# A zero-tile warm-up of TensorE from the first microsecond, and token tile 2's transposes moved behind the first slot

## The chip, the cores and the metric

The kernel runs on 1 core of a Trainium2 chip. The metric is the device time of one execution in microseconds (us), so less is better. Executions of one kernel differ by 1 to 3.5 us within a group of runs (2.1 us over 45 runs of the kernel before on one chip, 3.5 us over 62 on another), which is more than the change moves, so distributions are compared as well as medians.

## The reference, cut to what matters

A linear attention with cosine weights feeds a two-layer MLP with a squared ReLU.

```python
q_p = concat(relu(q) * cos_w, relu(q) * sin_w)      # 8 batches, 8 heads, 576 tokens, 64 -> 128 features
k_p = concat(relu(k) * cos_w, relu(k) * sin_w)
kv  = einsum('bhsf,bhsd->bhfd', k_p, v);  z = k_p.sum(axis=2)
x   = (q_p @ kv) / (q_p @ z + 1e-6)                 # -> 4608 tokens x 512
h   = x @ w_in                                      # 512 -> 2048
out = (relu(h) ** 2) @ w_out                        # 2048 -> 512
```

## The kernel before

All the work of TensorE is one stream of "slots". A batch has a first matmul stage (`gemm1`, against `w1sb`) and a second (`gemm2`, against `w2sb`). The attention of later batches is hung behind slots. Batch 0 has nothing in front of it to hide behind; its attention is the front that the change is about: k and v give `kz`, q is transposed (`tq`), multiplied (`num`), divided, transposed again (`tx`), and then slot 0 begins. `w1sb` and `w2sb` are the two weight matrices on the chip; each is loaded in four quarters through GpSimd's DMA queue. PSUM is the memory that the matmuls write their sums into; the tags `hps`, `yps` and `pa` in the code name groups of PSUM buffers, and in this kernel a buffer is used again only when VectorE or ScalarE has copied it out (in the first profile the fourth matmul of the second stage starts at 38.78 us, behind VectorE's copies, which take 0.77 us from 37.97).

```python
def warm(j):                                  # matmuls without use, to keep TensorE busy
    wm = ps_h.tile([P, 2, FP], F32, name="wm", tag="hps", bufs=2)
    for i in range(2):
        nc.tensor.matmul(out=wm[:, i, :], lhsT=ident[:, :],
                         rhs=kp_of(0, j)[:, i * HH : (i + 1) * HH, :], ...)

def gemm2(b, s):
    if b == 0:
        if s == 0:                            # four accumulators: two on the hps tag, two on yps
            yh = ps_h.tile([P, 2, DM], F32, name="yh", tag="hps", bufs=2)
            ...
            yps = ps_y.tile([P, DM], F32, name="yps", tag="yps", bufs=2)
        for hb in range(s * HB // 8, (s + 1) * HB // 8):
            for tt in range(J):
                gemm2_mm(b, tt, hb, ypss[b][tt])
        ...

load_batch(0, nc.sync, "kvq")
constants()
for j in range(NS):
    att_k(0, j)
    if j < J:
        warm(j)                               # 8 matmuls on the features of k
att_v(0, J - 1, nc.gpsimd, H - 1, H)          # GpSimd's first copy: it waits for v
...
for i in range(4):
    load_w1(i, 4)                             # GpSimd's queue, in this order
load_batch(1, nc.gpsimd, "qkv")
for i in range(4):
    load_w2(i, 4)
load_batch(2, nc.gpsimd, "qkv")
att_kv(0, 0); att_kv(0, 1)                    # kz
for j in range(J):
    warm(j)                                   # 8 more
...
att_qT_pe(0, 2)                               # transposes of token tile 2, in front of slot 0
att_qT_copy(0, 2, True)
for s in range(len(slots)):
    run(s)
```

Of the kernel before, what the change touches and what calls it, by code (L numbers as in the profile page):

```python
# [12 lines left out]
BF16 = mybir.dt.bfloat16  # L13

EPS = 1e-06
FP = 512
# [3 lines left out]
def kernel(  # L20
# [9 lines left out]
    nc = tc.nc  # L30
    P = nc.NUM_PARTITIONS
# [7 lines left out]
    J = S // P  # L39
    MAIN = J * P  # L40
    TAIL = S - MAIN
    HH = H // 2
# [3 lines left out]
    const = ctx.enter_context(tc.tile_pool(name="const", bufs=1))  # L46
# [35 lines left out]


    ident = const.tile([P, P], BF16, name="ident")
    cos_col = const.tile([P, J + 1], F32, name="cos_col")
    sin_col = const.tile([P, J + 1], F32, name="sin_col")

    def constants():
        sidx = const.tile([P, J + 1], F32, name="sidx")
        for p0, p1, c, n, base, mult in [  # L90
            (0, P, 0, J, 0, J),
            (0, TAIL, J, 1, MAIN, 1),
            (TAIL, P, J, 1, MAIN, 1),
        ]:
            nc.gpsimd.iota(
                sidx[p0:p1, c : c + n],
                pattern=[[1, n]],
                base=base,
                channel_multiplier=mult,
                allow_small_or_imprecise_dtypes=True,  # L100
            )
        bias_pi2 = const.tile([P, 1], F32, name="bias_pi2")
        nc.vector.memset(bias_pi2, math.pi / 2.0)
        theta_scale = (math.pi / 2.0) / S
        nc.scalar.activation(cos_col, sidx, ACTF.Sin, bias=bias_pi2[:], scale=-theta_scale)
        nc.scalar.activation(sin_col, sidx, ACTF.Sin, bias=0.0, scale=theta_scale)
        make_identity(nc, ident)
# [31 lines left out]
    def cached(tiles, key, shape, tag, bufs):  # L139
        if key not in tiles:  # L140
            tiles[key] = att.tile(shape, BF16, name=tag, tag=tag, bufs=bufs)
        return tiles[key]


    def kp_of(b, j):
        if j == J:
            return cached(kps, (b, 1), [P, HH, F], "kpt", 1)
        return cached(kps, (b, 0), [P, J, H, F], "kp", 1)[:, j]
# [12 lines left out]
    def xT_of(b, i):  # L161
        return cached(xts, (b, i), [P, KB, 2 * P], "xT", 4)
# [29 lines left out]
        else:  # L192
            copy(out=vx[:, j, h0:h1, 0:D], in_=piece("v", b, j)[:, h0:h1, :])  # L193

    def warm(j):

        wm = ps_h.tile([P, 2, FP], F32, name="wm", tag="hps", bufs=2)
        for i in range(2):
            nc.tensor.matmul(  # L199
                out=wm[:, i, :],  # L200
                lhsT=ident[:, :],
                rhs=kp_of(0, j)[:, i * HH : (i + 1) * HH, :],
                start=True,
                stop=True,
            )

    def fill(n):

        wm = ps_a.tile([P, 2, FP], F32, name="wm", tag="pa", bufs=1)
        for i in range(n):  # L210
            nc.tensor.matmul(  # L211
                out=wm[:, i % 2, :],
                lhsT=ident[:, :],
                rhs=kp_of(0, 0)[:, 0:HH, :],
                start=True,
                stop=True,
            )
# [52 lines left out]
    def att_qT_pe(b, j, apart=False):  # L270

        nh = H if j < J else HH
        tq = ps_y.tile([P, H, P], BF16, name="tq", tag="yps", bufs=2)
        tqs[b, j] = [tq[:, 0:HH, :]]
        if apart:
            hi = ps_h.tile([P, HH, P], BF16, name="tqh", tag="hps", bufs=2)
            tqs[b, j].append(hi)
        elif nh == H:
            tqs[b, j].append(tq[:, HH:H, :])
        for h in range(nh):  # L280
            nc.tensor.transpose(  # L281
                tqs[b, j][h // HH][:, h % HH, :], qp_of(b, j)[:, h, :], ident[:, :]
            )

    def att_qT_copy(b, j, both=False):
        qpTs[b, j] = []
        for i, tq in enumerate(tqs[b, j]):
            t = att.tile([P, HH, P], BF16, name=f"qpTp{i}", tag=f"qpTp{i}", bufs=5)
            copy = nc.scalar.copy if both and i else nc.vector.tensor_copy
            copy(out=t[:, :, :], in_=tq[:, :, :])  # L290
            qpTs[b, j].append(t)
# [46 lines left out]
            src = xs[b, i].rearrange("p k c -> p (k c)")  # L338
        nc.sync.dma_start_transpose(out=dst, in_=src)

    def att_x_pe(b, j, in_y=False):
        nk = KB if j < J else 2
        if in_y:
            tx = ps_y.tile([P, KB, P], BF16, name="tx", tag="yps", bufs=2)
        else:
            tx = ps_a.tile([P, KB, P], BF16, name="tx", tag="pa", bufs=1)
        for kb in range(nk):
            nc.tensor.transpose(tx[:, kb, :], x_of(b, j)[:, kb, :], ident[:, :])  # L348
        if j < J:
            dst = xT_of(b, j // 2)[:, :, j % 2 * P : (j % 2 + 1) * P]  # L350
        else:
            dst = xT_tails(b // 2)[:, b % 2].rearrange("p k g c -> p k (g c)")
        nc.scalar.copy(out=dst, in_=tx[:, 0:nk, :])



# [2 lines left out]
    def gemm1(b, s):  # L359
        if s == 0:  # L360
            gTs[b] = mlp.tile([P, HB, MAIN], BF16, name="gT", tag="gT", bufs=1)
        if s == 8:
            gTts[b // 2] = mlp.tile([P, HB, 2 * TAIL], BF16, name="gTt", tag="gTt", bufs=1)
        half = s // 4
        w, nh = (2 * P, 4) if half < 2 else (P, 8)
        h0 = s % 4 * nh
        hps = ps_h.tile([P, nh, w], F32, name="hps", tag="hps", bufs=2)

        step = P if (b, s) == (0, 0) else w
        for c in range(0, w, step):  # L370
            for i in range(nh):
                hb = h0 + i
                for kb in range(KB):
                    out = hps[:, i, c : c + step]
                    if half < 2:
                        rhs = xT_of(b, half)[:, kb, c : c + step]
                    else:
                        rhs = xT_tails(b // 2)[:, :, kb % 2, kb // 2, :]
                        out = out.rearrange("p (m c) -> p m c", m=2)
                    nc.tensor.matmul(  # L380
                        out=out,
                        lhsT=w1sb[:, kb, hb * P : (hb + 1) * P],
                        rhs=rhs,
                        start=(kb == 0),
                        stop=(kb == KB - 1),
                    )
        rt = mlp.tile([P, nh, w], BF16, name="rt", tag="rt", bufs=2)
        nc.scalar.activation(out=rt[:, :, :], in_=hps[:, :, :], func=ACTF.Relu)  # L388
        if half < 2:
            dst = gTs[b][:, h0 : h0 + nh, half * w : (half + 1) * w]  # L390
        else:
            dst = gTts[b // 2][:, h0 : h0 + nh, :]

        def square():
            nc.vector.tensor_tensor(out=dst, in0=rt[:, :, :], in1=rt[:, :, :], op=ALU.mult)  # L395

        return square
# [58 lines left out]
    for b in range(B):  # L456
        n = 8 + 2 * (b % 2)
# [4 lines left out]
    def at(s, fn, *args):  # L462
        after.setdefault(s, []).append((fn, args))
# [30 lines left out]
            at(kv[i], att_kv, b, i)  # L494


    at(0, att_qT_pe, 0, 3)
    at(0, att_num, 0, 2)
    at(0, att_qT_copy, 0, 3, True)
    at(0, att_div, 0, 2)  # L500
    at(1, att_x_pe, 0, 2, True)
    at(1, att_d, 0, 3)
    at(2, att_x_pe, 0, 3, True)
    at(12, att_feat, 0, J)
    at(17, att_t, 0, J)
    at(19, att_d, 0, J)
# [45 lines left out]
    with tc.manual_schedule():  # L552
        load_batch(0, nc.sync, "kvq")
        constants()
        for j in range(NS):
            att_k(0, j)
            if j < J:
                warm(j)
        att_v(0, J - 1, nc.gpsimd, H - 1, H)
        att_v(0, 0, nc.vector)  # L560
        att_v(0, 1, nc.scalar)
        att_v(0, 2, nc.vector)
        att_v(0, 3, nc.vector, 0, H - 1)
        att_v(0, J, nc.vector)
        for i in range(4):
            load_w1(i, 4)
# [3 lines that stand above are left out]
        load_batch(2, nc.gpsimd, "qkv")  # L570
        att_kv(0, 0)
        att_kv(0, 1)
        for j in range(J):
            warm(j)
        att_feat(0, 0)
        att_feat(0, 1)
        for j in range(2):
            att_qT_pe(0, j, True)
        for j in range(2):
            att_qT_copy(0, j, True)  # L580
            att_num(0, j, True)
        for j in range(2):
            att_div(0, j)
        att_feat(0, 2, "s")
        att_feat(0, 3, "s")
        for j in range(2):
            fill(4 - j)
            att_x_pe(0, j, True)
        att_feat(0, 2, "c")
        att_feat(0, 3, "c")  # L590
        att_qT_pe(0, 2)
        att_qT_copy(0, 2, True)
        for s in range(len(slots)):
            run(s)

# [28 lines left out]
```

## Time and profile before

| | before |
|---|---|
| time, first 3 runs | 300.6 us median, 300.25 to 301.1 |
| span of the profiled execution | 298.9 us |
| TensorE busy | 285.7 us, 96% |
| v of batch 0 landed | 10.84 us |
| kz (40 matmuls) | 2.25 us; batch 1's kz, same shapes, 1.20 us by the chain of waits, 1.36 us by the timeline (43.33 to 44.69) |
| first quarter of w2sb landed | 37.73 us |
| second stage begins | 37.80 us |

The table is to be read from the bottom. TensorE is dense from about 20 us on, so a gain in the front counts only if it still stands where the second stage begins, and there a transfer lands within 0.1 us of when it is wanted. The lines of the page and the trace are in the prediction.

### The profile page before, as it was taken

Reading aid. Unit: us, or ns where it says so; the run is one execution under the profiler, and the core shown is the slowest. Engines: PE = TensorE matmul, PEld = TensorE weight load, DVE = VectorE, ACT = ScalarE, POOL = GpSimd, SP = SyncE. Lnnn points to the kernel's source line nnn. Section 1 sums busy time; section 2 is a strip of 40 time slices with the busy share of each in tenths; the row PEclk is TensorE's granted clock in tenths of the full one; section 3 lists DMA queues with packets and bytes.
Section 4 is the critical chain, followed back from the end, with each engine's and each line's share of the span. In section 5 each row is a group of like instructions: output and inputs, shape, how many; then the busy total and the mean of one; then the engine's idle time right before and its main releaser. Section 6 shows DMA issues by size and latency. Waiting matters only on the chain.

```text
span 298.9 us, 6372 instructions
## 1 busy us (share of the span) xinstructions
PE 285.7 (96%) x2636; PEld 200.6 (67%) x2659; DVE 135.5 (45%) x330; ACT 154.0 (52%) x215; POOL 48.0 (16%) x79
## 2 busy tenths in 40 slices
PE   0899999999999999999999999999999999999995
PEld 0469855889556984589654884589754894589544
DVE  1455664465648386228730287227740273024100
ACT  3466753666838564655554555555563552255311
POOL 1554304751121002000021001100021000100000
PEclk9999999999999999999999999999999999999999
DMA  7999993999648996896779925798669013100021
GB/s 216 293 206 352 276 243 102 352 362 209 171 99 148 242 269 157 239 278 181 122 170 221 334 47 124 235 271 227 114 178 212 35 37 79 72 36 2 33 75 70
DMA packets 77069, 52.98 MB, mean 177 GB/s; under 512 B 52240, under 2 KB 71952, under 8 KB 77040
## 3 DMA queue, kind: packets, MB, share of 16 engines
q1 hardware_dynamic: 67120, 29.50, 42.7%
q0 software_dynamic: 9776, 22.94, 26.8%
q8 instruction: 21, 0.34, 0.4%
q10 hardware_dynamic: 144, 0.13, 0.1%
q14 instruction: 8, 0.07, 0.1%
HBM read 36.70 MB, written 9.44 MB: 154 GB/s over the span
## 4 chain that ended last, share of the span: by engine, by line
PE 93%; DMA 3%; ACT 1%; issue 1%; DVE 1%; SPq 1%; ACTq 0%
PE hps L380 42%; PE yps L415 39%; PE kz L238 4%; PE num L307 3%; DMA v<-in_v_dram 3%; PE yh L415 2%; PE tq L281 1%; PE wm L199 1%; PE tx L348 1%; PE wm L211 1%; SPq L69 0%; ACT qpTp L290 0%; ACT rt L388 0%; DVE qpTp L290 0%; DVE gTt L395 0%
## 5 line engine op out<-in xcount | busy, mean ns | idle before, releaser
L380 PEld LDWEIGHTS <-w1sb 128*128 128x128 bf16 x1296 | 113.0, 98 | 12.3
L380 PE MATMUL hps<-xT,w1sb 128*128 128x256 bf16 (+1 forms) x1040 | 117.8, 271 | 0.0
L415 PE MATMUL yps<-w2sb,gT 128*128 128x512 bf16 (+1 forms) x476 | 108.1, 372 | 1.4 <-DVE qpTp L290 0.2
L388 ACT ACTIVATE rt<-hps 128x1024 bf16<-128x1024 f32 x72 | 73.7, 1024 | 57.8 <-DVE gT L395 32.6
L415 PEld LDWEIGHTS <-gT 128*128 128x128 bf16 x528 | 49.5, 98 | 53.0 <-DVE qpTp L290 0.7
L395 DVE TENSOR_TENSOR gT<-rt 128x1024 bf16<-128x1024 bf16 x64 | 44.0, 688 | 84.5 <-ACT rt L388 84.5
L411 POOL DMA_DIRECT2D out_dram<-ysb x34 | 20.7, 610 | 176.5 <-ACT ysb L401 174.3
L401 ACT COPY ysb<-yps 128x512 f32<-128x512 f32 (+1 forms) x35 | 20.0, 575 | 56.1 <-PE yps L415 56.0
L179 ACT ACTIVATE qp<-q,sin_col 128x512 bf16<-128x512 f32 x32 | 21.9, 718 | 5.0 <-DMA q<-in_q_dram 5.0
L179 ACT ACTIVATE kp<-k,sin_col 128x512 bf16<-128x512 f32 x32 | 21.1, 713 | 3.2 <-DMA k<-in_k_dram 3.2
L321 DVE TENSOR_TENSOR x<-num,rden 128x512 bf16<-128x512 f32 x32 | 22.1, 691 | 1.1
L169 DVE TENSOR_SCALAR qp<-q,cos_col 128x512 bf16<-128x512 f32 x32 | 14.4, 489 | 11.7 <-DMA q<-in_q_dram 11.7
L169 DVE TENSOR_SCALAR kp<-k,cos_col 128x512 bf16<-128x512 f32 x32 | 15.1, 481 | 5.0 <-DMA k<-in_k_dram 5.0
L317 DVE TENSOR_SCALAR den<-num 128x8 f32<-128x8 f32 (+1 forms) x40 | 6.6, 165 | 22.3 <-PE num L307 22.1
L380 PE MATMUL hps<-xTt,w1sb 128*128 128x128 bf16 x256 | 15.3, 219 | 0.0
L415 PE MATMUL yps<-w2sb,gTt 128*128 128x512 bf16 x64 | 14.5, 379 | 0.0
L193 DVE CAST vext<-v 128x512 bf16<-128x512 f32 (+1 forms) x31 | 13.0, 425 | 2.7 <-DMA v<-in_v_dram 2.7
L238 PEld LDWEIGHTS <-kp 128*128 128x128 bf16 x256 | 10.3, 102 | 4.0 <-issue 1.6
L199 PE MATMUL wm<-kp,ident 128*128 128x512 bf16 x15 | 6.0, 553 | 7.2 <-ACT kp L179 7.0
L307 PEld LDWEIGHTS <-qpT 128*128 128x128 bf16 (+1 forms) x240 | 10.3, 100 | 3.3 <-issue 1.7
L307 PE MATMUL num<-kvz,qpT 128*128 128x65 bf16 (+1 forms) x240 | 11.7, 194 | 0.0
L238 PE MATMUL kz<-vext,kp 128*128 128x65 bf16 x256 | 10.7, 199 | 0.8 <-DVE vext L193 0.8
(56 smaller groups left out, 130.2 us busy)
## 6 DMA issues: line engine op xcount, KB each, us to landing
out_dram<-ysb POOLq DMA_DIRECT2D x28, 256.0 KB, 3.5
k<-in_k_dram SPq DMA_DIRECT2D x5, 1024.0 KB, 6.1
v<-in_v_dram SPq DMA_DIRECT2D x5, 1024.0 KB, 8.1
q<-in_q_dram SPq DMA_DIRECT2D x5, 1024.0 KB, 6.0
q<-in_q_dram POOLq DMA_DIRECT2D x3, 1024.0 KB, 13.5
k<-in_k_dram POOLq DMA_DIRECT2D x3, 1024.0 KB, 10.3
v<-in_v_dram POOLq DMA_DIRECT2D x3, 1024.0 KB, 9.8
w1sb<-in_moe_w_in_dram POOLq DMA_DIRECT2D x4, 512.0 KB, 8.2
```

The source lines that it names most:

```text
L169: nc.vector.tensor_scalar(out=dst[:, :, 0:D], in0=src, scalar1=0.0, scalar2=cos_col[:, j : j + 1], op0=ALU.max, op1=ALU.mult,)
L179: nc.scalar.activation(out=dst[:, :, D:F], in_=src, func=ACTF.Relu, scale=sin_col[:, j : j + 1])
L193: copy(out=vx[:, j, h0:h1, 0:D], in_=piece("v", b, j)[:, h0:h1, :])
L238: nc.tensor.matmul(out=kz[:, half, hh * E1 : (hh + 1) * E1], lhsT=lhsT, rhs=rhs, start=(j == 0 and hh == 0), stop=(j == J and hh == HH - 1),)
L307: nc.tensor.matmul(out=out, lhsT=lhsT, rhs=kvz[:, half * HH + hh, :], start=True, stop=True)
L321: nc.vector.tensor_tensor(out=x_of(b, j).rearrange("p (b k) (l d) -> p b k l d", b=n, l=2), in0=n4[:, :, :, 0:D].rearrange("p b (k l) d -> ...
L380: nc.tensor.matmul(out=out, lhsT=w1sb[:, kb, hb * P : (hb + 1) * P], rhs=rhs, start=(kb == 0), stop=(kb == KB - 1),)
L388: nc.scalar.activation(out=rt[:, :, :], in_=hps[:, :, :], func=ACTF.Relu)
L395: nc.vector.tensor_tensor(out=dst, in0=rt[:, :, :], in1=rt[:, :, :], op=ALU.mult)
L401: nc.scalar.copy(out=ysb[:, c0:c1], in_=acc)
L411: eng.dma_start(out=dst, in_=ysb[p0 : p0 + n, c0:c1])
L415: nc.tensor.matmul(out=acc, lhsT=lhsT, rhs=w2sb[:, hb, c0:c1], start=(hb == 0), stop=(hb == HB - 1))
```

## The change

The intent: in the first profile matmuls of 512 columns come every 0.43 us in the front and every 0.215 us from about 15 us on, so in that execution TensorE starts at half of its later speed. Below, full speed means 0.215 us for such a matmul, and the step to it is called the change of speed. The kernel before warms TensorE with k's features, which come at 7 us (first matmul at 6.96). The change warms it with a tile of zeros that is there at 1 us (first matmul at 1.19), so that kz should run at full speed. The transposes of token tile 2 leave the path to slot 0, and the copies of x that follow go to VectorE.

```diff
+    zeros = const.tile([P, FP], BF16, name="zeros")
+    nc.vector.memset(zeros, 0.0)
-    def warm(j):
+    def warm(n):
         wm = ps_h.tile([P, 2, FP], F32, name="wm", tag="hps", bufs=2)
-        for i in range(2):
+        for i in range(n):
             nc.tensor.matmul(
-                out=wm[:, i, :], lhsT=ident[:, :], rhs=kp_of(0, j)[:, ...], ...
+                out=wm[:, i % 2, :], lhsT=zeros[:, 0:P], rhs=zeros[:, :], start=True, stop=True
             )
...                                               # fill(): rhs=zeros too
-        step = P if (b, s) == (0, 0) else w
+        step = P if b == 0 and s % 4 == 0 else w
...
-    at(0, att_qT_pe, 0, 3)
-    at(0, att_num, 0, 2)
-    at(0, att_qT_copy, 0, 3, True)
-    at(0, att_div, 0, 2)
-    at(1, att_x_pe, 0, 2, True)
-    at(1, att_d, 0, 3)
-    at(2, att_x_pe, 0, 3, True)
+    for j in (2, 3):
+        at(0, att_qT_pe, 0, j)
+        at(0, att_qT_copy, 0, j, True)
+    at(1, att_d, 0, 2)
+    at(2, att_x_pe, 0, 2, True, nc.vector.tensor_copy)
+    at(2, att_d, 0, 3)
+    at(3, att_x_pe, 0, 3, True, nc.vector.tensor_copy)
...
+        warm(34)
         for j in range(NS):
             att_k(0, j)
-            if j < J:
-                warm(j)
...
-        for j in range(J):
-            warm(j)
+        warm(8)
...
-        att_qT_pe(0, 2)
-        att_qT_copy(0, 2, True)
```

More of the change, by code (lines that the diff above doesn't have):

```diff
@@ L193, in att_v @@
             copy(out=vx[:, j, h0:h1, 0:D], in_=piece("v", b, j)[:, h0:h1, :])
-    def warm(j):
+    def warm(n):
         wm = ps_h.tile([P, 2, FP], F32, name="wm", tag="hps", bufs=2)
-        for i in range(2):
+        for i in range(n):
             nc.tensor.matmul(
-                out=wm[:, i, :],
-                lhsT=ident[:, :],
-                rhs=kp_of(0, j)[:, i * HH : (i + 1) * HH, :],
-                start=True,
-                stop=True,
+                out=wm[:, i % 2, :], lhsT=zeros[:, 0:P], rhs=zeros[:, :], start=True, stop=True
             )
@@ L213, in fill @@
                 lhsT=ident[:, :],
-                rhs=kp_of(0, 0)[:, 0:HH, :],
+                rhs=zeros[:, :],
                 start=True,
@@ L339, in att_x, with att_x_pe @@
         nc.sync.dma_start_transpose(out=dst, in_=src)
-    def att_x_pe(b, j, in_y=False):
+    def att_x_pe(b, j, in_y=False, copy=nc.scalar.copy):
         nk = KB if j < J else 2
@@ L352, in att_x_pe @@
             dst = xT_tails(b // 2)[:, b % 2].rearrange("p k g c -> p k (g c)")
-        nc.scalar.copy(out=dst, in_=tx[:, 0:nk, :])
+        copy(out=dst, in_=tx[:, 0:nk, :])
     gTs, gTts, ypss = {}, {}, {}
```

## The prediction

> **What bounds the kernel now.** I read the page's slices first, then the chain of waits from 5 to 40 us, then the timeline of TensorE for the same stretch, then the DMA landings one issue at a time.
>
> ```profile
> PE   0899999999999999999999999999999999999995
> PEclk9999999999999999999999999999999999999999
> ```
>
> TensorE is 9 tenths busy in 37 of 40 slices. The 13.2 us that it is not busy (298.9 less 285.7) lie mostly in the first 7 us (6.96 us before its first matmul) and in the tail. So the kernel is one long TensorE stream, and a change to the front is worth what it moves the point from which that stream never waits again. The second row says full clock everywhere. The reader should not believe it for the front: the timeline shows matmuls of one shape at two speeds.
>
> ```profile
> 6.96 3.57 PE L199 MATMUL wm<-kp,ident 128*128 128x512 bf16 x8 [6.96 <-ACT kp L179]
> 11.34 1.92 PE L238 MATMUL kz<-vext,kp 128*128 128x65 bf16 x32 [0.80 <-DVE vext L193]
> 13.52 0.61 PE L199 MATMUL wm<-kp,ident 128*128 128x512 bf16 x1
> 14.35 1.82 PE L199 MATMUL wm<-kp,ident 128*128 128x512 bf16 x6 [0.22 <-issue]
> ```
>
> The first eight warm-up matmuls of 512 columns start every 0.43 us (their weight loads begin at 7.35, 7.77, 8.20, 8.63 us). Those at the end of the second group and those of the fillers at 18.2 us (four in the chain's 0.86 us) take 0.215 us each, half of it. The weight loads are last 0.42 us apart at 14.35 and 14.78 us and crowd from 15.15 us on, so this execution changed speed near 15.0 us. The 40 matmuls of kz lie wholly in the slow part: the chain gives them 2.25 us, and the same 40 of batch 1, at 43.49 us, 1.20 us.
>
> Now the chain up to the place where the two big matmul stages meet:
>
> ```profile
> 2.71 8.13 DMA v<-in_v_dram
> 11.34 2.25 PE kz L238 x40
> 14.35 1.82 PE wm L199 x6
> 16.66 1.08 ACT qpTp L290 x2
> 19.97 0.39 PE tx L348 x4
> 20.44 0.61 PE tq L281 x8
> 21.05 1.79 PE hps L380 x32
> 37.97 0.77 DVE qpTp L290 x2
> 38.78 0.39 PE yps L415
> ```
>
> The front is set by v landing at 10.84 us, then slow kz, then slow warm-up matmuls, then transposes, ScalarE copies and two divides, until the first slot of matmuls against w1sb. From 20.44 us the stream is dense (TensorE is busy 4.00 of each 4 us from 22 to 38), and the next real wait is at 38.2 us, where the fourth matmul of the second stage waits for a PSUM buffer that VectorE still copies out of.
>
> That second stage needs w2sb, and here lies the line that decides. The weights' tile, queried for its first issue alone:
>
> ```profile
> L122 POOL DMA_DIRECT2D w2sb<-in_moe_w_out_dram x1: 765/765/765, 28.8 to 28.8; - x1
> DMA to landing us min/median/max: 8.9/8.9/8.9
> ```
>
> Issued at 28.83, landed 8.9 us later: 37.73 us. The first matmul that reads it is here:
>
> ```profile
> 37.80 0.39 PE L415 MATMUL yh<-w2sb,gT 128*128 128x512 bf16 x1
> ```
>
> It starts 0.07 us after the landing, with no wait shown, because TensorE itself arrives then (its last eight transposes began at 37.33 us). Two chains meet at 37.8 us by chance or by tuning. A TensorE that comes earlier finds the weights not there.
>
> [...] 3.57 us of dense matmuls from 6.96 us did not suffice, and the change came only near 15 us. [...] in this trace the sixteen transposes from 16.18 us take 0.055 us each, and nothing slows after them. [...] w1sb, w2sb and the loads of batches 1 and 2 stand in one GpSimd queue, and from 11 to 45 us the DMA row is full, with some 205 GB/s while weights pass and some 380 GB/s in plain loads.
>
> **The change part by part.**
>
> Zero tile and 34 matmuls. VectorE gains one memset ahead of the small ones, a few tenths of a us, at about 0.9 us; it delays the bias constant, the table load and the two tables by as much, but they have until 6.19 us, when k lands, and end at 2.96 us now. TensorE can then start at about 1.3 us. [...] kz cannot start before 11.34 us anyway (v, then VectorE's cast). [...]
>
> kz. Its own work falls from 2.25 to 1.20 us. VectorE's last casts of v end near 12.3 us, so kz ends near 12.6 instead of 13.59 us: 1.0 us earlier.
>
> Eight warm-up matmuls after kz: 8 x 0.216 = 1.73 us, 12.6 to 14.3 us, in place of 2.6 us that end at 16.18. They now end before the q features are ready. Those are bound by q: issued at 5.60, landed 8.3 us later, 13.9 us. ScalarE's two sine features (1.33 us) run 13.97 to 15.3 in place of 14.12 to 15.45. The transposes of tile 1 can then follow at 15.35 and end by 15.8 (they ended at 16.64), and ScalarE's second copy, 0.53 us each behind the features and the first copy, ends at about 16.45 in place of 17.74. num, the two divides (1.05 us each on VectorE) and the transposes tx follow unchanged, so the last tx ends about 1.3 us earlier, at about 19.05 us in place of 20.36.
>
> Transposes of token tile 2 moved behind slot 0. They take 0.6 us in front of the first slot now, 0.45 where they fit behind other work. No instruction is saved, TensorE does them at 20.9 instead. The gain in dense work is about 0.15 us, and slot 4 pays some of it back: it is cut into columns of 128, 32 matmuls in 1.79 us in place of 16 in 1.75. The two x copies go from ScalarE (0.59 us) to VectorE (0.42 us), which between slots 0 and 4 has about 6.5 us of work in some 9 us. I find no new wait there; the tightest is x of tile 3, needed 0.9 us into slot 4, ready at about the same time.
>
> w1sb is not in the way: its quarters land at 16.8, 19.4, 22.1 and 25.0 us, and the four slots would want them at about 19.1, 21.8, 23.8 and 25.8 us.
>
> So TensorE comes to the second stage at 37.80 - 1.3 - 0.1 = about 36.4 us. And then it waits, until 37.73 plus some 0.05 us, because nothing in the change moves the DMA queue: GpSimd's program is the same, its first issue waits for v at 10.86 us, and later issues wait for earlier landings. The whole 1.4 us turns into a new wait. What is left is the wait behind it: now the fourth matmul starts at 38.78, where three at 0.216 from 37.80 would make it 38.45. With VectorE's copies done at about 37.3 it will no longer wait. Gain: 38.78 - 38.45 = 0.33 us. The later quarters of w2sb do not bind: the second lands at 40.3 (29.59 + 10.7), wanted 16 matmuls after 37.78, at 41.2.
>
> Sum: 0.33 us of 300.6, 0.1%.
>
> **The rivals.**
>
> One: the weights come earlier than I think, and the whole front gain of 1.4 us reaches the end: 299.2 us. For it speaks that TensorE shows no wait on w2sb now. Against it, the landing of 37.73 us and a DMA row that is full from 11 us on.
>
> Two: the warm-up does not work[...]. Then kz stays at 2.25 us and starts 4.5 us late behind 34 slow matmuls (1.3 + 34 x 0.427 = 15.8 us), the eight behind it are slow too (3.4 us, to 21.5 in place of 16.2), and the stream reaches the second stage some 5 us after 37.8: about 306 us. Against it: the thin stretch from 16.2 to 20.4 us holds its speed today[...].
>
> Three: [...] its change of speed decides when TensorE comes to 37.8 us; an earlier one is caught by w2sb at the value I predict, a later one loses up to some 0.8 us. Its three runs, 300.25 to 301.1, fit that. Then the gain against the median is 0.3 us, against a bad run 0.8, and the changed kernel's runs lie closer together, near the best of before.
>
> **Range and chances.** 300.6 - 0.33 gives 300.25; I say 300.2 us. 8 in 10: 299.6 (part of rival one, or a faster DMA queue) to 300.9 (nothing gained, a slow landing). Faster by 2% would be 6 us, over four times all that the front holds. Slower by 2% takes rival two at its worst. Chances: faster 0.01, within 2% 0.97, slower 0.02.
>
> **What would show it.** Right: kz's 40 matmuls in about 1.2 us near 11.4; the first w1sb matmul near 19.1; a new wait of TensorE of 1.0 to 1.5 us named w2sb, ending at 37.7 to 37.8; no wait for VectorE's copies behind it. Wrong: no w2sb wait, with an end 1 us or more earlier; w2sb issued or landed at another time; or matmuls of 0.43 us after 8 us.

## The result, and the profile after

The changed kernel took 300.58 us (median of 4 runs, 300.12 to 300.79), beside 300.65 us for the kernel before (4 runs). The ratio is 0.9995, with a 95% interval from 0.9977 to 1.0014: no difference. Ratios here and below are the mean time of one kernel's fast runs over that of the other's in the same rounds, so not quite the ratio of the medians quoted.

The timeline of the changed kernel's front (start us, length us, engine, line, operation, operands, count, and in brackets the idle time before it and what ended it):

```profile
1.19 8.96 PE L201 MATMUL wm<-zeros 128*128 128x512 bf16 x34 [1.19 <-DVE zeros L86]
...
4.15 5.50 PEld L201 LDWEIGHTS <-zeros 128*128 128x128 bf16 x26 [0.28 <-issue]
...
11.75 1.13 PE L236 MATMUL kz<-vext,kp 128*128 128x65 bf16 x32 [1.60 <-DVE vext L195]
...
12.81 0.30 PE L236 MATMUL kz<-vextt,kpt 64*128 64x65 bf16 x8
...
38.27 0.60 PE L413 MATMUL yh<-w2sb,gT 128*128 128x512 bf16 x2 [1.27 <-DMA w2sb<-in_moe_w_out_dram]
```

The warm-up does what it is for. Weight loads come every 0.43 us up to 4.15 us and then crowd, so TensorE was at full speed from about 4.3 us, and kz takes 1.36 us, 11.75 to 13.11, in place of 2.25. The last line is what became of it: TensorE stands still for 1.27 us in front of the second stage, waiting for w2sb. That wait was not in the first profile of before.

The chain of waits says the same from the other end (start us, us, what):

```profile
11.29 0.50 POOL vext L195
11.79 3.08 POOL w1sb L117 x4
14.87 13.74 DMA q<-in_q_dram
28.61 0.28 issue
28.89 0.61 POOL vt L69
29.50 8.73 DMA w2sb<-in_moe_w_out_dram
38.23 0.05 issue
38.27 0.60 PE yh L413 x2
```

Before 38 us there is no TensorE in it any more, where before it had a row of wm, kz, tq and hps. It follows GpSimd's queue: the copy of a piece of v, the issues of w1sb, batch 1's loads, w2sb. And the busy time on the page is more than before, for the same time:

```profile
PE 291.1 (97%) x2701; PEld 202.3 (68%) x2701; DVE 136.6 (46%) x333; ACT 153.0 (51%) x213; POOL 47.8 (16%) x79
```

TensorE's 5.4 us more of busy time (291.1 less 285.7) are mostly warm-up matmuls. They are the reason why busy time is no measure of progress here.

In this pair w2sb landed at 38.23 us after and 37.73 before, so the span was even 0.1 us longer. Nothing ties that to the change: v of batch 0, issued at the same time (2.70 us), landed at 11.24 against 10.84 us, and GpSimd's queue starts behind it. Over all profiles of this study v landed between 10.0 and 11.24 us with the new warm-up and between 10.8 and 11.0 us with the old, or with none.

### The profile page after: what moved, and what is told of

It is laid out like the page before. It is cut to its first block, busy times and chain, and to the rows that moved or that the text cites. A ratio compares the mean times of both kernels' runs of the same rounds, so it can differ in the third digit from the quotient of the medians.

```text
span 299.0 us, 6477 instructions
## 1 busy us (share of the span) xinstructions
PE 291.1 (97%) x2701; PEld 202.3 (68%) x2701; DVE 136.6 (46%) x333; ACT 153.0 (51%) x213; POOL 47.8 (16%) x79
## 4 chain that ended last, share of the span: by engine, by line
PE 86%; DMA 10%; POOL 1%; SPq 1%; issue 0%; ACT 0%; ACTq 0%
PE yps L413 40%; PE hps L378 38%; DMA q<-in_q_dram 5%; PE num L305 3%; DMA w2sb<-in_moe_w_out_dram 3%; DMA v<-in_v_dram 3%; PE kz L236 3%; PE yh L413 2%; POOL w1sb L117 1%; SPq L69 0%; PE tx L346 0%; PE tq L279 0%; POOL vt L69 0%; POOL vext L195 0%; SPq L64 0%
## 5 line engine op out<-in xcount | busy, mean ns | idle before, releaser
L413 PE MATMUL yps<-w2sb,gT 128*128 128x512 bf16 (+1 forms) x496 | 110.4, 372 | 0.0
L236 PEld LDWEIGHTS <-kp 128*128 128x128 bf16 x256 | 9.5, 97 | 4.4 <-issue 1.9
L201 PE MATMUL wm<-zeros 128*128 128x512 bf16 x42 | 10.9, 421 | 1.2 <-DVE zeros L86 1.2
L236 PE MATMUL kz<-vext,kp 128*128 128x65 bf16 x256 | 9.9, 193 | 1.6 <-DVE vext L195 1.6
```

Source lines behind the costliest of these rows:

```text
L236: nc.tensor.matmul(out=kz[:, half, hh * E1 : (hh + 1) * E1], lhsT=lhsT, rhs=rhs, start=(j == 0 and hh == 0), stop=(j == J and hh == HH - 1),)
L413: nc.tensor.matmul(out=acc, lhsT=lhsT, rhs=w2sb[:, hb, c0:c1], start=(hb == 0), stop=(hb == HB - 1))
```

## The experiments

All twelve ran; none was refused. e1 to e4 ran on one chip, e5 to e8 on a second, e9 to e11 on a third, e12 on a fourth, each beside runs of the kernel before on its chip (median 300.69, 300.43, 300.62 and 300.98 us). Compare times within a group only, ratios between groups.

The theory to test: w2sb's landing sets the end of the changed kernel, and the front's gain turned into a wait for it. The rival: the gain is lost elsewhere in the front, or behind another wait, and w2sb only happens to be named.

### e1 and e2: the wait taken away, the DMA queue untouched

Batch 0's second stage reads columns of w1sb, long landed, in place of w2sb. The results are wrong on purpose.

```diff
-            out=acc, lhsT=lhsT, rhs=w2sb[:, hb, c0:c1], ...
+        rhs = w1sb[:, hb % KB, hb // KB * DM :][:, c0:c1] if b == 0 else w2sb[:, hb, c0:c1]
+            out=acc, lhsT=lhsT, rhs=rhs, ...
```

e1, on the changed kernel:

> The changed kernel with the second matmul stage of batch 0 reading columns of w1sb (landed by 26 us) in place of w2sb: same count and shape of matmuls, same DMA queue, wrong result on purpose. Theory (TensorE waits for w2sb's first quarter): the wait of 1.27 us before the second stage goes, the stage starts near 36.9 us, and the time is 1.2 to 1.4 us under the changed kernel's, about 299.3 us, ratio about 0.995. Rival (the front gain is lost elsewhere, or a second wait close behind takes its place, for v or k of batch 1): the time stays within 0.3 us of 300.6.

Measured: 298.97 us (298.65 to 299.93), ratio 0.995. Against the changed kernel's own ratio of 0.9995 that is 0.0045 of 300 us, 1.35 us (give or take 0.7, from the two intervals), about the 1.27 us that the wait showed. In the timeline the second stage starts without a wait, and VectorE's copies, which the wait for w2sb had hidden, hold up its fourth matmul:

```profile
35.76 0.59 PE L414 MATMUL yh<-w1sb,gT 128*128 128x512 bf16 x2
36.77 0.39 PE L414 MATMUL yps<-w1sb,gT 128*128 128x512 bf16 x1 [0.20 <-DVE qpTp L288]
```

e2, on the kernel before:

> The kernel before with the same edit (w1sb in place of w2sb in batch 0's second stage). Theory: TensorE comes to the second stage at about 37.8 us by itself, so the time stays at 300.6, at most 0.3 us less on average if some executions arrive earlier and are caught by w2sb. Rival (w2sb already bounds the kernel before): it falls by about as much as the changed kernel does, 1 us or more.

Measured: 299.55 us (298.56 to 301.56, 22 runs), ratio 0.9971. This is a miss, and the most instructive one: the kernel before, whose profile showed no wait for w2sb, gains 0.9 us on average when that wait is taken away, close to the rival's 1 us. Its profile's timeline has kz at another speed than the first profile did:

```profile
11.42 1.49 PE L238 MATMUL kz<-vext,kp 128*128 128x65 bf16 x32 [0.66 <-DVE vext L193]
12.85 0.30 PE L238 MATMUL kz<-vextt,kpt 64*128 64x65 bf16 x8
13.08 1.90 PE L199 MATMUL wm<-kp,ident 128*128 128x512 bf16 x8
```

The 32 matmuls of kz take 1.49 us in place of 1.92, and the eight warm-up matmuls behind them 1.90 in place of some 2.7. So in this execution the change of speed came already during kz. In the chain of that execution kz doesn't appear; q does, which sets the front:

```profile
5.75 8.60 DMA q<-in_q_dram
14.37 0.73 ACT qp L179
15.15 0.40 PE tq L281 x4
```

The rival theory for the kernel before thus became: executions of the kernel before are of two kinds, an early kind in which TensorE is at full speed in or before kz, so that q and not kz sets the front and TensorE waits for w2sb, and a late kind, which the first profile caught. e4, e7, e9 and e10 bear on that.

### e3 and e4: the weights earlier

```diff
-        load_batch(1, nc.gpsimd, "qkv")
-        for i in range(4):
+        load_batch(1, nc.gpsimd, "q")
+        load_w2(0, 4)
+        load_batch(1, nc.gpsimd, "kv")
+        for i in range(1, 4):
             load_w2(i, 4)
```

e3, the changed kernel with this order:

> The changed kernel with the first quarter of w2sb put ahead of k and v of batch 1 in the GpSimd queue; right result. Theory: that quarter lands near 31 us, the wait for it goes; the second quarter, which lands no earlier than before (40.3 to 41.0 us), is now wanted at about 36.9 + 16 x 0.216 = 40.4 us, so a wait of up to 0.6 us shows there; time 299.3 to 300.0. v of batch 1 lands near 38 us and is wanted by 42. Rival (the queue's order is not what matters): 300.6.

Measured: 299.6 us (298.77 to 300.01), correct, ratio 0.9962 (0.9949 to 0.9975). The wait for w2sb is gone; what stands at the start of the second stage is VectorE's copy out of the PSUM buffers that two of its accumulators need, in the chain of waits:

```profile
35.72 0.46 PE tq L279 x8
36.21 0.77 DVE qpTp L288 x2
37.02 0.39 PE yps L413
```

The second quarter made no wait of 0.6 us: its matmuls ran on at 39.86 us with 0.03 us lost.

e4, the kernel before with this order:

> The kernel before with the same order of the queue. Theory: nothing was waiting for w2sb's first quarter, so 300.6 within 0.3. Rival: it falls by 0.7 us or more, and then the reorder alone would do what the warm-up is credited with.

Measured: 300.01 us, ratio 0.9987 (0.9974 to 1.0). That is 0.68 us under before by the medians and 0.4 us by the ratio: more than the theory allowed and just short of the rival's 0.7, because there are two groups: 14 of 22 runs lie from 299.09 to 300.18 us, 8 from 300.72 to 301.26. The profiled execution is of the second group (its chain of waits):

```profile
11.49 2.25 PE kz L238 x40
13.74 2.92 PE wm L199 x8
```

kz and the warm-up run at half speed, as in the first profile of before. So the reorder alone helps the first group, and e3, with the new warm-up, lacks the second.

### e5: the changed kernel again, for its spread

> The changed kernel once more, beside the kernel before on one chip, for the spread. Theory (the end is set by w2sb's landing, in every execution of the changed kernel and in the fast ones of the kernel before): 300.2 to 300.6 median, a ratio of 0.998 to 1.000, no execution above 301.0, none under 299.3; the kernel before again shows a group at 300.7 to 301.4 that the changed kernel lacks. Rival (front gain lost at random): the changed kernel spreads over 299 to 301.4 like the kernel before.

Measured: 300.48 us (299.94 to 302.14, 14 runs) against 300.43 us, ratio 0.9999 (0.998 to 1.0018). The median and the ratio are as expected, and the profiled execution waits 1.3 us for w2sb; the spread is not: two runs are above 301.0 us, one of them at 302.14, and the kernel before's group cannot be told from its noise on this chip. Some spread should have been expected: in the six profiles with the queue in its old order (before, after, e1, e2, e5, e9) w2sb's first quarter landed between 37.73 and 38.66 us. The few slow runs here have no profile; what they waited for is open.

### e6 and e7: each part alone, with the weights early

e6 is e4 plus the zero tile; the transposes stay in front:

```diff
+        warm(34)                                  # on zeros, as in the change
         for j in range(NS):
             att_k(0, j)
-            if j < J:
-                warm(j)
...
-        for j in range(J):
-            warm(j)
+        warm(8)
```

e7 is e3 with the old warm-up put back:

```diff
-        warm(34)
         for j in range(NS):
             att_k(0, j)
+            if j < J:
+                warm(j)                           # on k's features, as before
...
-        warm(8)
+        for j in range(J):
+            warm(j)
```

> Only the zero-tile warm-up, transposes left in front, with the first quarter of w2sb ahead of k and v so that the front's gain can show. Theory: the warm-up carries nearly all of the change: 299.6 to 299.8, without the slow group at 300.7 to 301.3 that e4 has. Rival (the moved transposes carry it): about 300.0 with that group.

Measured: 299.55 us (299.13 to 299.98, 21 runs), ratio 0.9965, no run of the slow group.

> Only the moved transposes (with the cut of slot 4 and the x copies on VectorE), old warm-up, same early quarter of w2sb. Theory: 0.1 to 0.15 us under e4, about 299.9, two groups about 1.2 us apart as in e4. Rival: as e3, 299.6 with one group.

Measured: 299.39 us (298.91 to 301.33, 22 runs), ratio 0.9967. Eighteen runs lie from 298.91 to 300.15 us and four from 301.15 to 301.33. The expectation missed: the median is 0.5 us below the 299.9 named, and the groups are 1.9 us apart, not 1.2. One of the four slow runs, at 301.21 us, shows a mean granted clock of 0.994. Its profile is of the fast group, and in its timeline the old warm-up has kz at full speed:

```profile
6.84 3.45 PE L199 MATMUL wm<-kp,ident 128*128 128x512 bf16 x8 [6.84 <-ACT kp L179]
11.37 1.13 PE L238 MATMUL kz<-vext,kp 128*128 128x65 bf16 x32 [1.08 <-DVE vext L193]
```

The times alone give only the difference of the two parts in an early execution: e7's fast group has its median at 299.34 us, e6 at 299.55. The traces separate them. From the last `tx` in front of slot 0 to the second stage TensorE takes 17.82 us in e6 (18.84 to 36.66) and 17.61 us in e12, described below (18.85 to 36.46), whose front is the same but for the moved transposes; so these, with the cut of slot 4 and the copies on VectorE that go with them, are worth 0.2 us where nothing hides them. That leaves about nothing for the zero tile in an execution of the early kind. In the slow groups it is worth what parts them from the fast ones, 1.4 us between the medians in e4 (8 of 22 runs) and 1.9 us in e7 (4 of 22). It takes away the late kind, not time. That each slow group is the late kind rests on one profile, e4's, and on e10.

### e9: a second profile of the kernel before

> The kernel before, unchanged, for one more profile, since its first one caught an execution whose matmuls changed speed only at 15 us and e2, e4, e7 show that the same front often changes before or within kz. If this execution is of the early kind (4 in 5 of those seen), the theory expects kz in 1.2 to 1.6 us, TensorE at the second stage near 37.0 us, and a wait of 0.3 to 1.2 us for w2sb there, time 300.0 to 300.5. Rival (before never waits for w2sb): no such wait. If it is of the late kind it tells nothing new: kz in 2.25 us and no wait.

Measured: 301.24 us, one run. The execution is of the early kind, and the wait for w2sb is there, in the timeline:

```profile
36.41 0.61 PE L281 MATMUL tq<-ident,qp 128*128 128x128 bf16 x8
...
38.71 0.39 PE L415 MATMUL yh<-w2sb,gT 128*128 128x512 bf16 x1 [1.68 <-DMA w2sb<-in_moe_w_out_dram]
```

TensorE was done at 37.0 us, as in the changed kernel, and waited 1.68 us, longer than expected, because w2sb landed at 38.66 us. That is also why an execution of the fast front took 301.24 us. The new wait of the changed kernel was not new: the kernel before had it in this execution, whose front was fast.

The profiles on record also show that nothing after the start of the second stage parts these executions. In the eleven whose later work is the same (before, after, e1 to e7, e9, e10) the span is the start of the second stage's fourth matmul plus 260.06 to 260.13 us: 38.78 and 298.9 us in before, 38.94 and 299.0 in after, 39.37 and 299.5 in e9, 36.77 and 296.9 in e1. (In after, e5 and e9 that matmul is the second of a pair, 0.215 us behind the first.) Two things set its start. Where VectorE's copies bind (before, e1 to e4, e6, e7, e10), it comes 0.98 to 1.02 us after the first matmul of the second stage; where w2sb binds (after, e5, e9), 0.71 to 0.72 us after w2sb's landing. So in these profiles the end is set by the later of two times: TensorE's arrival plus 1.0 us, and w2sb's landing plus 0.7 us.

### e10: no warm-up ahead of kz

```diff
         for j in range(NS):
             att_k(0, j)
-            if j < J:
-                warm(j)
```

> e4 with the first eight warm-up matmuls taken out and nothing in their place: kz is then TensorE's first work. Theory (the slow group is the executions whose matmuls change speed after kz): every execution is now of that kind, one group at 300.8 to 301.6, median 301.2, none under 300.3. Rival (the slow group has another cause, such as late landings): two groups as in e4, most of them at 299.1 to 300.2.

Measured: 301.38 us (300.44 to 302.51, 19 runs), ratio 1.002 (1.0006 to 1.0034). No run is as fast as e4's first group, though the runs spread over 2.1 us and not over the 0.8 us expected; what parts them is open. In the profile kz takes the slow time again:

```profile
11.33 1.92 PE L238 MATMUL kz<-vext,kp 128*128 128x65 bf16 x32 [11.33 <-DVE vext L193]
13.18 0.40 PE L238 MATMUL kz<-vextt,kpt 64*128 64x65 bf16 x8
```

So in these runs the early kind comes from a warm-up ahead of kz, and the slow group of e4 and e7 is what remains when the change of speed comes only behind kz, as in e4's profile (1.92 us for the same 32 matmuls). e10 ran on another chip than e4, so only the direction against its own kernel before is to be read: e4 is below 1, e10 above it.

### e8, e11 and e12: towards a version that beats both

e8 is e3 with the first slot of the second stage ordered so that the accumulators on the free PSUM tiles go first.

```diff
-            for hb in range(s * HB // 8, (s + 1) * HB // 8):
-                for tt in range(J):
-                    gemm2_mm(b, tt, hb, ypss[b][tt])
+            hbs = range(s * HB // 8, (s + 1) * HB // 8)
+            groups = [range(J)] if s else [(0, 1), (2, 3)]
+            for tts in groups:
+                for hb in hbs:
+                    for tt in tts:
+                        gemm2_mm(b, tt, hb, ypss[b][tt])
```

> e3 with the first four matmuls of the second stage put on the two PSUM tiles of the hps pool, so that those that wait for VectorE's transposed copies come later. Theory: the wait of about 0.55 us for those copies (36.2 to 37.0 us in e3) goes, but the second quarter of w2sb, landing at about 39.9 us or later, is then wanted at 39.7, so it gains 0.1 to 0.5 us over e3: 299.1 to 299.5. Rival: no gain, since that quarter was at its limit in e3 already: 299.6.

Measured: 299.44 us (298.6 to 299.93), ratio 0.9958 (0.9943 to 0.9973), not to be told from e3. The wait for VectorE is gone, and part of it came back as the next wait for weights, in the timeline:

```profile
39.69 0.59 PE L413 MATMUL yps<-w2sb,gT 128*128 128x512 bf16 x2
40.44 0.59 PE L413 MATMUL yh<-w2sb,gT 128*128 128x512 bf16 x2 [0.16 <-DMA w2sb<-in_moe_w_out_dram]
```

Pairs of matmuls begin 0.43 us apart; here it is 0.75.

e11 puts the second quarter of w2sb ahead of v of batch 1 and, since v then lands later, batch 1's kz, divides and transposes a slot later.

```diff
-        load_batch(1, nc.gpsimd, "kv")
-        for i in range(1, 4):
-            load_w2(i, 4)
+        load_batch(1, nc.gpsimd, "k")
+        load_w2(1, 4)
+        load_batch(1, nc.gpsimd, "v")
+        load_w2(2, 4)
+        load_w2(3, 4)
...
-        kv=(10, 10), d=(11, 13, 15, 17, 21), ... x=(12, 14, 16, 18, 22),
+        kv=(11, 11), d=(12, 14, 16, 17, 21), ... x=(13, 15, 17, 18, 22),
-                at(x[j], att_x_pe, b, j)
+                at(x[j], att_x_pe, b, j, x[j] in (17, 18))
```

> e8 with the second quarter of w2sb ahead of v of batch 1 too, and batch 1's kz one slot later, its first divides and transposes with it. Theory: the second quarter lands near 37 us and no longer binds, v lands near 40.5 us and is wanted at 43; 299.0 median, 0.3 to 0.5 us under e8's ratio, about 0.994 to 0.995 of before. Rival: the moved slots of batch 1 bring a wait of their own, near slots 12 to 18 (44 to 58 us), and the time is 299.4 or more.

Measured: 301.42 us (300.6 to 303.14), ratio 1.0043: a miss for the theory, and the rival's case. The timeline shows the new wait where batch 1's first stage begins:

```profile
51.98 1.07 ACT L399 COPY ysb<-yh 128x512 f32<-128x512 f32 x2 [2.27 <-PE yh L413]
52.21 0.39 PE L346 MATMUL tx<-ident,x 128*128 128x128 bf16 x4
52.94 1.09 ACT L399 COPY ysb<-yps 128x512 f32<-128x512 f32 x2
53.89 0.63 ACT L351 COPY xT<-tx 128x512 bf16<-128x512 bf16 x1
54.57 1.91 PE L378 MATMUL hps<-xT,w1sb 128*128 128x256 bf16 x16 [1.98 <-ACT xT L351]
```

The transposes are done at 52.6 us, but ScalarE makes four output copies first, and TensorE waits 1.98 us for the fifth. Moving a transpose into the slot just before its consumer put it behind the store.

The size of the miss is not all from this wait. Four of the nine runs, those from 301.9 us up, show a mean granted clock of 0.994, the other five 0.999 or 1.0. Without the runs at 0.994 on either side the means are 300.92 us against 300.56, 0.1% over the kernel before and not 0.4%. That the clock made those runs slow is not shown.

e12 is e11 with that copy on VectorE and the consuming slot cut into columns of 128, so that its first half doesn't need it.

```diff
-        step = P if b == 0 and s % 4 == 0 else w
+        step = P if (b == 0 and s % 4 == 0) or (b, s) == (1, 0) else w
...
-                at(x[j], att_x_pe, b, j, x[j] in (17, 18))
+                at(x[j], att_x_pe, b, j, x[j] in (17, 18),
+                   nc.vector.tensor_copy if x[j] == 15 else nc.scalar.copy)
```

> e11 with its new wait mended: in e11 the second batch's first slot waited 2.0 us for a copy that ScalarE made behind four output copies; here VectorE makes that copy, and the slot is cut into columns of 128 so that its first half doesn't need it. Theory: the 2.0 us wait goes, the ratio to before falls from 1.0043 by about 0.0065 to 0.996 to 0.998, no better than e3 and e8, since TensorE's second stage starts at the same 36.8 us as there; if the second quarter of w2sb was a real bound in e8, 0.994 to 0.995. Rival (another wait of the moved slots remains, near 54 to 62 us): 0.999 or more.

Measured: 299.16 us (299.0 to 299.39, 6 runs) against 300.98 us, correct, ratio 0.9943 (0.993 to 0.9956). It is the best of all correct versions by its ratio, and its runs lie within 0.4 us; its interval still overlaps e3's and e8's. TensorE's whole list of waits is now in the front:

```profile
PE wm L201 <- DVE zeros L86: 1.2, 1, 1.2
PE kz L236 <- DVE vext L195: 1.2, 1, 1.2
PE tq L279 <- DVE qp L171: 0.3, 1, 0.3
PE num L305 <- ACT qpTp L288: 0.2, 1, 0.2
```

The second quarter of w2sb, issued at 25.89 us, lands 11.0 us later, at 36.9 us, 3 us before it is wanted. The ratio fell by 0.0100 from e11's, more than the wait of 1.98 us is worth (0.0066); without e11's four runs at the lower clock it is 0.007. It lies in the second branch of what was expected, that the quarter was a real bound in e8. e8's trace shows that bound, 0.32 us lost (0.75 less 0.43); the times do not tell e8 and e12 apart.

## Why the prediction was right or wrong

**The time and its range**: right. 300.2 was predicted with 299.6 to 300.9, and 300.58 measured. The range allowed for no gain at all, so that it held is no evidence for the 0.33 us.

**Zero tile, change of speed and kz**: right. That matmuls on zeros would bring full speed before kz was the author's estimate; no profile from before the change had such matmuls. The change of speed came near 4.3 us, and between 4.1 and 6.9 us in the seven other profiles with the zero tile; the 34 matmuls ended by 10.2 us. kz took 1.36 us by the timeline, as long as batch 1's kz by the same view; the predicted 1.20 is that kz by the chain.

**The arrival at the second stage**: right to within the landings. Predicted about 36.4 us, measured 38.27 - 1.27 = 37.0, with slot 0 at 19.47 in place of 19.05 us. The 37.0 is the end of the last transposes. They start at 36.40, and where nothing is waited for the next matmul starts 0.45 us later (e6), so TensorE could have started at about 36.85. The difference is v and q of batch 0, which landed about 0.4 us later in that execution. In e1's profile, with v at 10.0 us, TensorE arrived at 35.8.

**The new wait for w2sb**: right, 1.27 us where 1.0 to 1.5 was predicted, and shown to be what bounds the end by e1, where taking it away gave 1.35 us. Its end was predicted for 37.7 to 37.8 and came at 38.27, later by w2sb's own landing.

**The term that was mis-sized is the 0.33 us of gain**, the difference between 38.78 and 38.45 us. Measured were 0.07 us between the first medians and a ratio of 0.9999 in e5, both inside the noise. The term was worked out from one profile, which is a special case twice over. First, it is of the late kind, in which TensorE comes to the second stage last and waits for VectorE's copies there. In the early kind (the profiles of e2, e7 and e9, and by their times the fast groups of e4 and e7, 14 of 22 and 18 of 22 runs) TensorE could start there at 36.65 to 36.9 us; with the queue in its old order it waits for w2sb as the changed kernel does (1.68 us in e9), and VectorE's copies are done by then. There the change has nothing to gain. Second, its w2sb landed at 37.73 us, the earliest of six landings; with 38.0, as in e2 and e5, the fourth matmul of the changed kernel starts at 38.7 us and even that late execution gains 0.1 us (an estimate from the 0.71 us above). The third rival of the prediction described this spread, but took the late kind for the median; the runs say that it is the minority. Its sign that the changed kernel's runs lie closer together did not show: they spread over 2.2 us in e5. The same fault stands in e2's expectation, 0.3 us at most where 0.9 came.

**Rival one** (the front's gain reaches the end, 299.2 us) was refuted as a forecast, and e3 shows that it comes near to the truth with one transfer moved: 1.0 us of the 1.4 by the ratios (0.9962 against 0.9995). **Rival two** (the warm-up does not work, and kz stays at 2.25 us) was refuted by the timeline: kz in 1.36 us, no slow matmul after 4.3 us, and none after 7 us in any of the eight profiles with the zero tile.

**What stays open**: what e5's slowest runs waited for, what spreads e10's runs, and why w2sb's first quarter landed anywhere from 37.7 to 38.7 us with the same order of issues.

## What to carry to other kernels

Before speeding up the front of a stream, look up the landing of the next transfer that the stream will need: if it lands where it is wanted today, the gain becomes a wait, and the transfer has to be moved with it, as in e3 (0.4% under the kernel before; the moved transfer alone gave 0.1% in e4, the faster front alone nothing in e5). One profile shows one execution: where the runs fall into groups, find out which group the profile is of before a wait, or the lack of one, is taken from it. And when a step is moved towards its consumer, look at what else stands in the queue of the engine that finishes it (e11).

## What the traces show of the change of speed and of the loads

- In the eight profiles with the zero tile, TensorE is dense from 1.19 us and at full speed 2.9 us (e8) to 5.7 us (e5) later, 3.1 us in the changed kernel's first. In e2 and e9 the speed changed in kz, after a dense stretch of 3.57 us and an idle gap of 0.65 us, and in the first profile of before the same dense stretch did not suffice and the change came 4.5 us after its end, behind kz and some of the second eight warm-up matmuls.
- Eight matmuls of 512 columns ahead of kz (3.57 us in e4's profile, 3.45 in e7's) left 8 of 22 (e4) and 4 of 22 executions (e7, one of them at the clock of 0.994) in the slow group, and 34 left none of 29 (e3, e6).
- The 16 transposes of the changed kernel at 15.29 us came 0.055 to 0.06 us apart, as fast as before, and nothing behind them was slow: the 32 matmuls of slot 0 took 1.79 us in both profiles.
- The profile's row of granted clock does not show this change of speed: it read 9 tenths in all 40 slices of before, while matmuls in two of them took twice their time.
- One and the same load spreads: that of v, issued at the same time (2.7 us), landed between 10.0 and 11.24 us. GpSimd's queue starts behind it, and the front moved with it: TensorE came to the second stage at 35.8 us in e1, with v at 10.0, and at 37.0 us in the changed kernel's first profile, with v at 11.24.
